# Scores' exponentials in pairs of turns: one ScalarE operation over two copied score pairs, and VectorE's exponential in other steps

## The chip, the cores and the metric

The kernel runs on one NeuronCore of a Trainium2 chip. It uses TensorE (PE; PEld is its weight load), VectorE (DVE), ScalarE (ACT), GpSimd (POOL) and the DMA queues, most of them issued from SyncE (SP). The metric is the device time of one execution in microseconds; the time before is the median of three runs, 1421.75 us (1420.74 to 1422.44).

## The reference

Two attention layers over the same shapes (2048 tokens, width 576, 32 heads of 18), their outputs side by side:

```python
def _A_ref(x, wq, wk, wv, wo):      # one key and value head for all 32 query heads
    q = heads(x @ wq); k = x @ wk; v = x @ wv
    p = softmax(q @ k.T * 18 ** -0.5)          # 32 heads x 2048 x 2048
    return concat(p @ v) @ wo
def _B_ref(x, wq, wk, wv, wo, beta):           # four segments of 512 tokens
    for s in range(4):
        p = softmax(causal(qs @ ks.T * scale))  # 32 heads x 512 x 512
        o = g * (phi(qs) @ M) / (phi(qs) @ z + 1e-6) + (1 - g) * (p @ vs)
        M, z = M + phi(ks).T @ vs, z + sum(phi(ks))
    return concat(o) @ wo
return concatenate([a, b], axis=-1)
```

The work of this case is A's softmax: 32 heads x 2048 x 2048 exponentials of fp32 scores.

## The kernel before

A first stage projects both inputs to queries, keys and values, splits them into exact parts and stores them in DRAM. It ends about 290 us into the span. All that follows is one long schedule written out by hand for PE, ACT and DVE (`manual_schedule`): each of these engines executes in the order in which the program text issues, and waits in place.

**Blocks.** A's work is cut into 32 blocks (4 chunks of 512 queries by 8 groups of 4 heads). B's is cut into 32 blocks too (segment and group of 4 heads), placed in pairs behind certain A blocks: `after` lists the A block behind which each of 16 pairs stands, and the pairs stand behind blocks 0, 1, 2, 3, 4, 8, 9, 10, 12, 16, 17, 18 and 20 (two pairs behind 0, 1 and 3). From block 21 on, A blocks follow each other.

**Pairs and turns.** An A block has 16 key tiles of 128 keys. For each key tile and each pair of heads (`pr`), two matmuls (upper and lower half of the rows) make a score tile E of 128 x 2 x 512 fp32 in PSUM (`scores`, L906). Three E buffers of two banks each (`psE`) take turns. A block has 32 such score pairs; they are issued in ten turns of three and one last turn of two (`turns`). What a score pair then meets depends on its place in the turn: the first and third are read by ACT straight from PSUM (exponential into P, L937); the middle one is copied by DVE into W in SBUF (L934), which frees its E buffer, and ACT takes its exponential from W last in the turn. In the last turn of two the second is the copied one. B's blocks have two turns of three each.

One score pair of each A block (key tile 0, `pr` 1, the middle of turn 0) gets its exponential from DVE alone (`exponentials`, L886): a first operation reads E, and eight more steps of 128 x 1024 each follow, one a turn (`slow`), skipped in turns where a block's output is read. Its result PD is used late, at place 12 of its pair's 16 key tiles (`LATE`).

**One turn** issues, in this order: the scores of its pairs (PE) with copies (DVE), the exponentials (ACT: first, third, middle), one fill step (PE: a few matmuls of an output projection into F, L770, or of B's memory, L826, with a copy to osb or o by DVE now and then), a DVE step, and the products of the turn two before (PE: P with V into O, L967; three half pairs a turn). A block's end adds a copy of O (oe, L976) and its store. `due` issues work on weights, sums and loads whose time has come.

**Tiles.** P has 9 buffers, W 2 (one pair each), PD, n, q one each (128 x 1024); stacks of queries (`load_stackA`): st0 for the first, then stA with 2 buffers, each for two blocks, asked for when the one before begins.

**Tail.** After the last block, A's last two output projections run from halves that ACT and DVE make of the weighted heads into P tiles (`halve_heads`), 3.2 us of PE for each of ten.

Of the kernel before, what the change touches and what calls it, by code (L numbers as in the profile page):

```python
# [1 line left out]

# [5 lines left out]
F32 = mybir.dt.float32  # L8
F32R = mybir.dt.float32r
BF = mybir.dt.bfloat16  # L10
I32 = mybir.dt.int32
AF = mybir.ActivationFunctionType
ALU = mybir.AluOpType
AX = mybir.AxisListType
# [4 lines left out]
S, D, H, DH = 2048, 576, 32, 18  # L19
NSEG, L = 4, 512  # L20
C = 512
NCH = S // C
NKT = S // 128
# [21 lines left out]


LOG2 = SCALE * 1.4426950408889634
ROUND = 1.5 * 2.0 ** 23
POLY = [753.2113037109375, 522.0861206054688, 180.93731689453125, 41.808597564697266, 7.287727355957031]
C5_BITS = 984482944.0  # L50

BY_DVE = ((0, 1),)
LATE = (12,)
QALL = [(slice(0, 36, 2), 0), (slice(1, 36, 2), 1), (slice(36, 54), 0)]
CA = 618
# [16 lines left out]
def attention_pair_kernel(ctx, tc, a_xT, a_w, a_wo, b_xT, b_w, b_wo, b_beta, ident_d, hmask_d, bmask_d, cmask_d, sel_d, zmask_d, selx_d, sely_d, out):  # L72
# [813 lines left out]

    def exponentials(p, e):

        n = pp.tile([128, 2, 512], F32, name="n", bufs=1)
        q = pp.tile([128, 2, 512], F32, name="q", bufs=1)  # L890
        v = nc.vector
        v.tensor_scalar(p, e, LOG2, -116.0, op0=ALU.mult, op1=ALU.max)
        steps = [
            lambda: v.tensor_scalar(n, p, ROUND, ROUND, op0=ALU.add, op1=ALU.subtract),
            lambda: v.tensor_tensor(p, p, n, op=ALU.subtract),
            lambda: v.scalar_tensor_tensor(q, p, POLY[4], p, op0=ALU.add, op1=ALU.mult),
        ]
        for a in POLY[3:0:-1]:
            steps.append(lambda a=a: v.scalar_tensor_tensor(q, q, a, p, op0=ALU.add, op1=ALU.mult))  # L899
        steps += [  # L900
            lambda: v.tensor_scalar(n.bitcast(I32), n, 2.0 ** 23, C5_BITS, op0=ALU.mult, op1=ALU.add),
            lambda: v.scalar_tensor_tensor(p, q, POLY[0], n, op0=ALU.add, op1=ALU.mult),
        ]
        slow.extend((now[0] + 2 + i, p, step) for i, step in enumerate(steps))

    def scores(it, pr, copied):  # L906

        ab, c, hg, kt = it
        st = stacks[ab, c, hg // 2]
        h = 2 * (hg % 2) + pr  # L910
        e = psE.tile([128, 2, 512], F32, name="E")
        dve = ab == "A" and (kt, pr) in BY_DVE
        p = pp.tile([128, 2, 512], F32, name="PD" if dve else "P", bufs=1 if dve else PBUFS)
        state[it, pr] = p
        n = 512 if ab == "A" else 512 - 128 * kt if kt < 2 else 384
        if ab == "A":
            for j, r0 in enumerate(HALF):
                rows = slice(r0, r0 + KR)
                nc.tensor.matmul(e[:, j], kstA[rows, 128 * kt : 128 * kt + 128], st[rows, h, :], start=True, stop=True)  # L919
            if (kt, pr) in BY_DVE:  # L920
                exponentials(p, e)
                return lambda: None
        else:
            for k, c0 in BKEYS[kt]:
                ks = slice(128 * k, 128 * k + 128)
                for j, r0 in enumerate(HALF):
                    rows = slice(r0, r0 + KR)
                    nc.tensor.matmul(  # L928
                        e[:, j, c0 : c0 + 512 - 128 * k], st[rows, 4 + h, ks], st[rows, h, 128 * k :], start=True, stop=True
                    )  # L930
        src = e
        if copied:
            src = pp.tile([128, 2, 512], F32, name="W", bufs=2)
            nc.vector.tensor_copy(src[:, :, :n], e[:, :, :n])  # L934

        def exponential():
            nc.scalar.activation(p[:, :, :n], src[:, :, :n], AF.Exp, scale=SCALE)  # L937
# [76 lines left out]
    def due(k, most=2, heavy=2):  # L1014

        cost = 0

        near = [its[n][0] for t in turns[k : k + 3] for n, pr in t]
# [68 lines left out]
    with tc.manual_schedule(engines={ENG.PE, ENG.Activation, ENG.DVE}):  # L1087
# [1 line left out]


        for n, b in enumerate(blocks):
            ms = [m for m in range(len(its)) if block_of[m] == n]
            items = [(m, k) for m in ms for k in range(2)]
            for out_, cut in ((turns, len(items) // 3), (prods, len(items) // 3 - 2)):
                at_ = split(len(items), cut)
                out_ += [items[a:z] for a, z in zip(at_, at_[1:])]
        at(ASK + 4, 0, lambda: True, lambda k: load_qf(2))

        def halve(hi, lo, src):
# [10 lines left out]
        wparts = []  # L1110
        for k in range(len(turns) + 2):
            now[0] = k
            exps = [scores(its[n], pr, i == 1) for i, (n, pr) in enumerate(turns[k])] if k < len(turns) else []
            for i in (0, 2, 1) if len(exps) == 3 else range(len(exps)):
                exps[i]()
            if memory is None:
                run_fill()
            elif k >= ASK and all(its[n][0] == "A" for n, pr in turns[k]) and next(memory, None) is None:
# [12 lines left out]
            due(k)  # L1131
            if k == len(turns):
                halve_w(0)
            for n, pr in turns[k] if k < len(turns) else []:
# [17 lines left out]

        def halve_heads(key, t):
            R = RT[t]
            x = halves_of[key, t] = pp.tile([128, 2, 512], F32R, name="P", bufs=PBUFS)
            halve(x[:R, 0], x[:R, 1], parts[key][:R, t])

        def multiply(key, t, dst):
# [25 lines left out]
        for n, key in enumerate(rows):  # L1184
            end = key == rows[-1]
            banks = [psE.tile([128, 2, 512], F32, name="E") for _ in range(3)]
            dst = [bk[:, hf, :288] for bk in banks for hf in range(2)]
            dst += [psO.tile([128, C], F32, name=nm)[:, :288] for nm in ("O", "F")]
            for t in range(5):
                while end and weighed[key] <= t:  # L1190
                    due(k, 4)
                    k += 1
                if end and t == 4:
                    halve_heads(key, t)
                multiply(key, t, dst)
            for i in range(4):
                if end:
                    osb = pp.tile([128, 2, 512], F32, name="P", bufs=PBUFS)[:, :, :288]
                elif i < 2:
                    osb = pp.tile([128, 2, 512], F32, name="W", bufs=2)[:, :, :288]  # L1200
# [62 lines left out]
```

## Time and profile before

| what | value |
|---|---|
| median of three runs | 1421.75 us |
| span of the profiled execution | 1419.2 us |
| first and last exponential of scores (L937) | 292.0 and 1376.8 us |
| exponentials by ACT from E, from W | 800, 384 |
| copies of scores by DVE (L934) | 384 |
| busy share of PE, ACT, DVE, POOL | 99%, 85%, 73%, 18% |

The profiled execution took 1419.2 us from its first to its last instruction; the runs' median is 2.55 us above that, and any sum made on the trace is carried over with this difference. Rows of a timeline read: start in us from the span's beginning, length in us, engine, line, operation, what it writes and reads, how many were merged (x2: two operations, the length from the first's start to the last's end), and in brackets how long the engine sat idle before it and what ended that. Rows of waits read: engine and line, what it waited for: us in total, times, longest. Rows of groups read: busy us, mean ns of one, then idle us before them by releaser. A matmul's end is modelled, so a turn on PE is best measured from start to start.

### The profile page before, as it was taken

What the parts mean: (1) busy time and instruction counts of PE and PEld (TensorE: products, weight loads), DVE (VectorE), ACT (ScalarE), POOL (GpSimd) and SP (SyncE); (2) the same over time, 40 slices, a digit from 0 to 9 for tenths busy, and PEclk for the clock granted to TensorE, in tenths of its full rate; (3) what the DMA queues carried; (4) which work ended last, traced back from release to release, by engine and by line L of the source; (5) the groups of instructions that cost most, each with busy time, mean ns of one, the idle gap of its engine ahead of it and who ended that gap; (6) DMA issues with size and microseconds to landing.
All of it is one profiled execution on the core that took longest, in us unless ns stands there. A gap on an engine that the chain in (4) does not pass through costs nothing.

```text
span 1419.2 us, 40029 instructions
## 1 busy us (share of the span) xinstructions
PE 1403.0 (99%) x17132; PEld 843.0 (59%) x17132; DVE 1034.8 (73%) x1221; ACT 1205.2 (85%) x1447; POOL 249.8 (18%) x326
## 2 busy tenths in 40 slices
PE   9999999999999999999999999999999999999998
PEld 6788888745555555555555555555555555555558
DVE  6656456467787778777777888777778877887773
ACT  4543434489999999999999999999999999999991
POOL 2431000003313214231110160131012400100002
PEclk9999999999999999999999999999999999999999
DMA  9766547457574535332312543232104121110013
GB/s 282 254 218 187 166 146 220 167 171 219 157 211 159 172 113 165 91 109 77 111 58 69 167 129 91 70 107 73 51 34 135 64 75 47 59 44 18 9 60 111
DMA packets 90720, 172.63 MB, mean 122 GB/s; under 512 B 14576, under 2 KB 22889, under 8 KB 90110
## 3 DMA queue, kind: packets, MB, share of 16 engines
q1 hardware_dynamic: 84122, 160.01, 36.0%
q0 software_dynamic: 1664, 4.78, 1.3%
q10 hardware_dynamic: 4752, 5.24, 1.1%
q8 instruction: 135, 2.21, 0.7%
q14 instruction: 47, 0.39, 0.1%
HBM read 99.32 MB, written 70.67 MB: 120 GB/s over the span
## 4 chain that ended last, share of the span: by engine, by line
PE 67%; ACT 9%; issue 2%; DVE 1%; DMA 0%; POOL 0%; ACTq 0%; DVEq 0%
PE O L967 30%; PE E L919 20%; PE F L770 11%; ACT P L937 9%; PE E L928 3%; PE E L1164 2%; PE F L826 1%; DVE W L934 0%; DMA oA<-oe 0%; PE F L1164 0%; PE O L1164 0%; DMA sm<-oA 0%; POOL P L942 0%; DVE osb L794 0%; DVE o L831 0%
## 5 line engine op out<-in xcount | busy, mean ns | idle before, releaser
L937 ACT ACTIVATE P<-E 128x1024 f32<-128x1024 f32 (+1 forms) x800 | 783.8, 1066 | 11.8 <-PE E L919 11.7
L934 DVE COPY W<-E 128x1024 f32<-128x1024 f32 (+1 forms) x384 | 461.1, 1201 | 178.7 <-PE E L919 121.6
L967 PE MATMUL O<-P,VA 128*32 128x256 f32 x7936 | 508.3, 379 | 0.0
L937 ACT ACTIVATE P<-W 128x1024 f32<-128x1024 f32 (+1 forms) x384 | 429.2, 1118 | 3.6 <-DVE W L934 3.4
L967 PEld LDWEIGHTS O<-P,VA 128*32 128x32 f32 x7936 | 262.5, 110 | 146.5 <-issue 5.7
L919 PE MATMUL E<-stA,kstA 56*128 56x512 f32 x1920 | 329.1, 439 | 2.0 <-DVE W L934 1.0
L919 PEld LDWEIGHTS E<-stA,kstA 56*128 56x128 f32 x1920 | 154.8, 184 | 178.3 <-ACT P L937 114.0
L942 POOL TENSOR_SCALAR_AFFINE_SELECT P<-P 128x256 f32<-128x256 f32 (+1 forms) x192 | 94.7, 493 | 474.2 <-ACT P L937 441.7
L758 POOL TENSOR_TENSOR o<-o,rb 126x512 f32<-126x512 f32 (+1 forms) x55 | 85.5, 1573 | 408.0 <-PE E L919 156.2
L770 PE MATMUL F<-woB,o 126*32 126x192 f32 (+1 forms) x1920 | 127.4, 338 | 0.3 <-DVE osb L794 0.3
L899 DVE SCALAR_TENSOR_TENSOR q<-q,PD 128x1024 f32<-128x1024 f32 x96 | 119.3, 1243 | 0.0
L967 PE MATMUL O<-P,vseg 128*32 128x256 f32 (+2 forms) x1536 | 81.4, 344 | 0.0
L770 PEld LDWEIGHTS F<-woB,o 126*32 126x32 f32 (+1 forms) x1920 | 38.2, 108 | 70.5 <-issue 62.7
L976 DVE COPY oe<-O 128x512 f32<-128x512 f32 x64 | 44.3, 692 | 40.2 <-PE O L967 39.5
L249 PE MATMUL pj<-xh,wBl 128*126 128x512 f32 x180 | 72.4, 403 | 0.0
L249 PE MATMUL pj<-xh,wBh 128*126 128x512 f32 x180 | 71.8, 400 | 0.0
L118 ACT CAST qp<-pj 126x512 fp32r<-126x512 f32 (+1 forms) x54 | 30.9, 584 | 46.6 <-DVE kmB L447 32.6
L770 PE MATMUL F<-woA,o 126*32 126x192 f32 (+1 forms) x960 | 63.9, 338 | 0.0
L928 PE MATMUL E<-stB 56*128 56x256 f32 (+3 forms) x512 | 61.8, 347 | 1.7 <-ACT P L937 1.1
L967 PEld LDWEIGHTS O<-P,vseg 128*32 128x32 f32 x1536 | 48.9, 109 | 24.1 <-issue 1.6
L119 DVE TENSOR_TENSOR qp<-pj,qp 126x512 fp32r<-126x512 f32 (+1 forms) x54 | 36.6, 685 | 35.8 <-ACT qp L118 35.7
L928 PEld LDWEIGHTS E<-stB 56*128 56x128 f32 x512 | 38.6, 185 | 32.1 <-ACT P L937 22.4
(194 smaller groups left out, 1401.9 us busy)
## 6 DMA issues: line engine op xcount, KB each, us to landing
stB<-kB SPq DMA_DIRECT2D x96, 144.0 KB
stB<-qB SPq DMA_DIRECT2D x32, 288.0 KB
stA<-qA SPq DMA_DIRECT2D x30, 288.0 KB
oA<-oe SPq DMA_DIRECT2D x32, 256.0 KB
oB<-oe SPq DMA_DIRECT2D x32, 256.0 KB
qA<-qp SPq DMA_DIRECT2D x16, 504.0 KB
kB<-qp SPq DMA_DIRECT2D x16, 504.0 KB
qB<-qp SPq DMA_DIRECT2D x16, 504.0 KB
```

Of the source, the lines that this page charges most:

```text
L119: hold(nc.vector.tensor_tensor(qp[:R, 1, :n], src, qp[:R, 0, :n].bitcast(F32), op=ALU.subtract))
L249: nc.tensor.matmul(dst, w[:, c0 : c0 + M], x, start=i == 0, stop=i == len(ops) - 1)
L758: return lambda: tc.keep_in_program_order(nc.gpsimd.tensor_tensor(dst, a, b, op=op))
L770: nc.tensor.matmul(dst[32 * j : 32 * j + 32], parts[ab, c][: RT[t], t, r0 : r0 + 32], wo[ab][: RT[t], t, c0 : c0 + n], start=start, stop=stop,
L899: steps.append(lambda a=a: v.scalar_tensor_tensor(q, q, a, p, op0=ALU.add, op1=ALU.mult))
L919: nc.tensor.matmul(e[:, j], kstA[rows, 128 * kt : 128 * kt + 128], st[rows, h, :], start=True, stop=True)
L928: nc.tensor.matmul(e[:, j, c0 : c0 + 512 - 128 * k], st[rows, 4 + h, ks], st[rows, h, 128 * k :], start=True, stop=True)
L934: nc.vector.tensor_copy(src[:, :, :n], e[:, :, :n])
L937: nc.scalar.activation(p[:, :, :n], src[:, :, :n], AF.Exp, scale=SCALE)
L942: nc.gpsimd.affine_select(diag, diag, pattern=[[0, 2], [0, m], [1, 128]], base=0, channel_multiplier=-1, compare_op=ALU.is_ge, fill=0.0)
L967: nc.tensor.matmul(o[32 * j : 32 * j + 32, q0 : q0 + n], v, p[:, j % 2, p0 : p0 + n], start=m == hf == 0, stop=last and hf == 1,)
L976: nc.vector.tensor_copy(osb, o)
```

## The change

The turns of an A block are written out by kind. Key tiles are taken in threes (i, i+1, i+2), two turns for each: the first has (i, pair 0), (i+2, pair 0), (i, pair 1); the second (i+1, pair 0), (i+2, pair 1), (i+1, pair 1). The middle ones are still copied by DVE, but into the two halves of one W of 128 x 4 x 512, and one ACT operation of 2048 columns takes both exponentials into the tile PW (4 x 512), last in the second turn. The third key tile of the first three (2) gives one pair to DVE's exponential (role "D", now `pr` 0, the middle of turn 0) and one that is copied and has a 1024-column exponential of its own. The last turn of two (key tile 15) has both pairs read from PSUM by ACT (role "E"). B's turns keep their order; their middle pairs lie in halves of W and PW too, with an exponential each.

In ACT's order, a block's exponentials before: two in turn 0, three in turns 1 to 9 (E, E, W), two in turn 10 (E, W). After: two (E, E) in turn 0, three (E, E, W) in turn 1, two in turns 2, 4, 6 and 8, two and a 2048-column one in turns 3, 5, 7 and 9, two (E, E) in turn 10. In DVE's order, nine copies a block for ten; DVE's exponential is one operation on 1024 columns and twelve on 512 (of these four are bit operations on whole words, eight have two operands), issued in groups of 3, 2, 3, 2 and 2, in turns 0, 2, 3, 4 and 5. On PE, the products of the moved key tiles change place; number and order of scores, fills and products by turn stay.

P has 6 buffers for 9; W and PW have 2 of two pairs each; n and q have half the size; st0 serves every second stack and stA has one buffer. In the tail four of the halves stand in PW.

```diff
-PBUFS = 9
+PBUFS = 6
-BY_DVE = ((0, 1),)
+BY_DVE = ((2, 0),)
 LATE = (12,)
...
-        st = pp.tile([128, 4, C], F32R, name="stA", bufs=2)
+        st = st0 if q4 % 2 == 0 else pp.tile([128, 4, C], F32R, name="stA", bufs=1)
...
     def exponentials(p, e):
...
+        u, w = (pp.tile([128, 512], F32, name=nm, bufs=1) for nm in "nq")
+        v, stt = nc.vector, nc.vector.scalar_tensor_tensor
+        v.tensor_scalar(p.bitcast(U32), e, EXP_A, EXP_B, op0=ALU.mult, op1=ALU.add)
+        ops = []
+        for t in (p[:, 0], p[:, 1]):
+            y = t.bitcast(U32)
+            ops += [
+                lambda y=y: v.tensor_scalar(u.bitcast(U32), y, MANTISSA, ONE_BITS, op0=ALU.bitwise_and, op1=ALU.bitwise_or),
+                lambda y=y: v.tensor_scalar(w.bitcast(U32), y, EXPONENT, None, op0=ALU.bitwise_and),
+                lambda t=t: stt(t, u, POLY[0], u, op0=ALU.add, op1=ALU.mult),
+                lambda t=t: stt(t, t, POLY[1], u, op0=ALU.add, op1=ALU.mult),
+                lambda t=t: stt(t, t, POLY[2], t, op0=ALU.add, op1=ALU.mult),
+                lambda t=t: stt(t, t, POLY[3], w, op0=ALU.add, op1=ALU.mult),
+            ]
+        for i, (lo, hi) in enumerate(((0, 3), (3, 5), (5, 8), (8, 10), (10, 12))):
+            slow.append((now[0] + 2 + i, p, ops[lo:hi]))
+
+    box = {}
 
-    def scores(it, pr, copied):
+    def scores(it, pr, role):
...
+        if role in (0, 1):
+            if role == 0:
+                box["W"] = pp.tile([128, 4, 512], F32, name="W", bufs=2)
+                box["P"] = pp.tile([128, 4, 512], F32, name="PW", bufs=2)
+            w, p = (box[nm][:, 2 * role : 2 * role + 2] for nm in "WP")
...
-        if copied:
-            src = pp.tile([128, 2, 512], F32, name="W", bufs=2)
+        if role in (0, 1):
+            src = w
             nc.vector.tensor_copy(src[:, :, :n], e[:, :, :n])
+            if ab == "A" and kt != BY_DVE[0][0]:
+                both = [box[nm] for nm in "PW"]
+                return (lambda: nc.scalar.activation(*both, AF.Exp, scale=SCALE)) if role else lambda: None
...
+            if b[0] == "A":
+                for i in range(0, NKT - 1, 3):
+                    x = "D" if i + 2 == BY_DVE[0][0] else 0
+                    turns.append([(m0 + i, 0, "E"), (m0 + i + 2, 0, x), (m0 + i, 1, "E")])
+                    turns.append([(m0 + i + 1, 0, "E"), (m0 + i + 2, 1, 0 if x else 1), (m0 + i + 1, 1, "E")])
+                turns.append([(m0 + NKT - 1, 0, "E"), (m0 + NKT - 1, 1, "E")])
+            else:
+                turns.append([(m0, 0, "E"), (m0, 1, 0), (m0 + 1, 0, "E")])
+                turns.append([(m0 + 1, 1, "E"), (m0 + 2, 0, 1), (m0 + 2, 1, "E")])
...
-            exps = [scores(its[n], pr, i == 1) for i, (n, pr) in enumerate(turns[k])] if k < len(turns) else []
+            exps = [scores(its[n], pr, role) for n, pr, role in turns[k]] if k < len(turns) else []
             for i in (0, 2, 1) if len(exps) == 3 else range(len(exps)):
                 exps[i]()
...
-                slow.pop(0)[2]()
+                for op in slow.pop(0)[2]:
+                    op()
```

More of the change, by code (lines that the diff above doesn't have):

```diff
@@ L1 @@
+import math
 from contextlib import ExitStack, nullcontext
@@ L11 @@
 I32 = mybir.dt.int32
+U32 = mybir.dt.uint32
 AF = mybir.ActivationFunctionType
@@ L887, in exponentials @@
     def exponentials(p, e):
[L889 to L904, printed above, removed]
-    def scores(it, pr, copied):
+        u, w = (pp.tile([128, 512], F32, name=nm, bufs=1) for nm in "nq")
[16 more added lines that the diff above has]
+    def scores(it, pr, role):
         ab, c, hg, kt = it
@@ L911, in scores @@
         e = psE.tile([128, 2, 512], F32, name="E")
-        dve = ab == "A" and (kt, pr) in BY_DVE
-        p = pp.tile([128, 2, 512], F32, name="PD" if dve else "P", bufs=1 if dve else PBUFS)
+        if role in (0, 1):
[4 more added lines that the diff above has]
+        else:
+            dve = role == "D"
+            p = pp.tile([128, 2, 512], F32, name="PD" if dve else "P", bufs=1 if dve else PBUFS)
         state[it, pr] = p
@@ L919, in scores @@
                 nc.tensor.matmul(e[:, j], kstA[rows, 128 * kt : 128 * kt + 128], st[rows, h, :], start=True, stop=True)
-            if (kt, pr) in BY_DVE:
+            if role == "D":
                 exponentials(p, e)
@@ L1016, in due @@
         cost = 0
-        near = [its[n][0] for t in turns[k : k + 3] for n, pr in t]
+        near = [its[t[0][0]][0] for t in turns[k : k + 3]]
         heavy *= "B" not in near
@@ L1091, in attention_pair_kernel @@
         for n, b in enumerate(blocks):
[L1092 to L1096, printed above, removed]
+            m0 = block_of.index(n)
+            if b[0] == "A":
[4 more added lines that the diff above has]
+                turns.append([(m0 + NKT - 1, 0, "E"), (m0 + NKT - 1, 1, "E")])
+            else:
+                turns.append([(m0, 0, "E"), (m0, 1, 0), (m0 + 1, 0, "E")])
+                turns.append([(m0 + 1, 1, "E"), (m0 + 2, 0, 1), (m0 + 2, 1, "E")])
+            halves = [(m, hf) for m in range(len(its)) if block_of[m] == n for hf in range(2)]
+            at_ = split(len(halves), len(halves) // 3 - 2)
+            prods += [halves[a:z] for a, z in zip(at_, at_[1:])]
         at(ASK + 4, 0, lambda: True, lambda k: load_qf(2))
@@ L1117, in attention_pair_kernel @@
                 run_fill()
-            elif k >= ASK and all(its[n][0] == "A" for n, pr in turns[k]) and next(memory, None) is None:
+            elif k >= ASK and its[turns[k][0][0]][0] == "A" and next(memory, None) is None:
                 memory = None
@@ L1133, in attention_pair_kernel @@
                 halve_w(0)
-            for n, pr in turns[k] if k < len(turns) else []:
+            for n, pr, role in turns[k] if k < len(turns) else []:
                 it = its[n]
@@ L1154, in halve_heads @@
             R = RT[t]
-            x = halves_of[key, t] = pp.tile([128, 2, 512], F32R, name="P", bufs=PBUFS)
+            if key == rows[0] or t == 4:
+                x = pp.tile([128, 2, 512], F32R, name="P", bufs=PBUFS)
+            else:
+                if t % 2 == 0:
+                    box["x"] = pp.tile([128, 4, 512], F32R, name="PW", bufs=2)
+                x = box["x"][:, 2 * (t % 2) : 2 * (t % 2) + 2]
+            halves_of[key, t] = x
             halve(x[:R, 0], x[:R, 1], parts[key][:R, t])
@@ L1199, in attention_pair_kernel @@
                 elif i < 2:
-                    osb = pp.tile([128, 2, 512], F32, name="W", bufs=2)[:, :, :288]
+                    osb = pp.tile([128, 4, 512], F32, name="W", bufs=2)[:, :2, :288]
                 else:
```

7 lines of the change are left out of this document (4 added, 3 removed).

## The prediction

> **What bounds the kernel now.** I read the page's head first, then the busy time by stretches, then the waits of one regular stretch, and last the two timelines of one block.
>
> ```profile
> span 1419.2 us, 40029 instructions
> ```
> ```profile
> 1113.00:1346.00 233.00, 232.91 (x3287) 121.77 (x3276) 184.98 (x180) 231.03 (x250) 10.13 (x8) 1.00 0.13 40
> ```
> ```profile
> PEld E L919 <- ACT P L937: 19.8, 57, 0.4
> ...
> ACT P L937 <- PE E L919: 1.5, 6, 0.3
> ```
>
> The second row covers eight A blocks (length, then busy time of PE, PE's weight loads, DVE, ACT, POOL; clock; DMA): PE is busy 232.91 of 233.00 us and ACT 231.03. Clock and DMA are out of it. The waits of 1172 to 1346 us show that two engines share the bound: PE waits 57 times for an exponential to give a score buffer back, ACT six times, once a block, for scores. So the order of two chains decides, not a sum of busy times. One block on each:
>
> ```profile
> 1201.14 1.21 PE L919 MATMUL E<-stA,kstA 56*128 56x512 f32 x6
> 1202.27 0.53 PE L770 MATMUL F<-woA,o 72*32 72x192 f32 x8
> ...
> 1204.03 0.96 PE L919 MATMUL E<-stA,kstA 56*128 56x512 f32 x6
> 1204.92 0.53 PE L770 MATMUL F<-woA,o 126*32 126x192 f32 x8
> ...
> 1206.68 0.97 PE L919 MATMUL E<-stA,kstA 56*128 56x512 f32 x6
> ...
> 1223.64 0.53 PE L770 MATMUL F<-woA,o 126*32 126x192 f32 x8
> ...
> 1226.42 0.53 PE L770 MATMUL F<-woA,o 126*32 126x192 f32 x8
> ...
> 1228.18 0.73 PE L919 MATMUL E<-stA,kstA 56*128 56x512 f32 x4
> ...
> 1230.17 1.17 PE L919 MATMUL E<-stA,kstA 56*128 56x512 f32 x6
> ```
> ```profile
> 1201.28 1.21 ACT L937 ACTIVATE P<-W 128x1024 f32<-128x1024 f32 x1
> 1202.23 2.09 ACT L937 ACTIVATE P<-E 128x1024 f32<-128x1024 f32 x2
> 1204.57 1.94 ACT L937 ACTIVATE P<-E 128x1024 f32<-128x1024 f32 x2 [0.25 <-PE E L919]
> 1206.40 1.06 ACT L937 ACTIVATE P<-W 128x1024 f32<-128x1024 f32 x1
> 1207.35 1.94 ACT L937 ACTIVATE P<-E 128x1024 f32<-128x1024 f32 x2
> 1209.15 1.08 ACT L937 ACTIVATE P<-W 128x1024 f32<-128x1024 f32 x1
> ...
> 1223.88 2.06 ACT L937 ACTIVATE P<-E 128x1024 f32<-128x1024 f32 x2
> ```
>
> Read the constants off these rows. **PE:** a turn that waits for nothing takes 2.65 us (1204.03 to 1206.68): 0.90 from its scores to its fill (F), 1.76 from fill to the next scores. The short last turn takes 1.99 (1228.18 to 1230.17). **ACT:** by their ends (1206.51, 1207.46, 1209.29) exponentials follow each other at 0.915 us from PSUM and 0.945 from W. Scores that begin when ACT is free end their first exponential 1.57 us later (1204.03 to 1206.51 less one 0.915). **Handover:** PE's fill at 1226.42 comes 0.48 us after the exponential that ended at 1225.94, on whose buffer the turn's third scores waited.
>
> With these constants a block goes turn by turn: fill = the later of scores + 0.90 and the previous turn's last PSUM exponential + 0.48; next scores = fill + 1.76; first exponential ends at the later of the preceding exponential's end + 0.915 and scores + 1.57. For the kernel before, started with its own 1.13 us from scores to fill and a last exponential that ends at 1202.49 (1.35 into the block), this gives 29.00 us; the rows give 29.03. The steps therefore describe this kernel, and I use them on the new one.
>
> **The change, part by part.**
>
> *Wide exponentials.* The rest of ACT's price per instruction comes from two sizes:
>
> ```profile
> 904.23 1.68 ACT L937 ACTIVATE P<-E 128x768 f32<-128x768 f32 x2
> 905.62 1.03 ACT L937 ACTIVATE P<-W 128x768 f32<-128x768 f32 x1
> ```
>
> Two exponentials of 768 columns follow at 0.695 us each, against 0.90 for 1024 by starts (1207.35 to 1209.15, two): 0.82 ns a column, 0.84 us per 1024. So 0.105 of W's 0.945 us is fixed, and I take 0.945 + 0.84 = 1.79 us for 2048 columns. No row shows that size; the ends are 1.70 (no fixed part) and 1.89 (nothing saved). Four an A block save 0.42 us of ACT, the block's last middle pair read from PSUM instead of W another 0.03: 0.45 a block, 14 over 32 blocks.
>
> The Trainium skill (Perfetto Trace Analysis, Optimizing Scalar/DVE Operations) gives 93 ns for ScalarE's fixed part on SBUF and says that grouping helps a saturated engine; by it the wide operation would take 1.80, and the block below would be some 0.03 us longer, as an estimate. The trace agrees on the size. The same section says that long instructions on an engine that causes bubbles elsewhere are better broken up; that is this forecast's case.
>
> *When ACT's work falls due.* This is the part that decides. A block's turns gave ACT 2, 3, 3 ... 3, 2 exponentials. Now turn 0 has 2, turn 1 has 3, turn 2 has 2, turn 3 has 2 and the wide one at its very end, and so on in twos. Over turns 0 to 3 ACT has about nine short operations for four PE turns, so it must idle; what it hasn't done comes back as wide operations later, and ACT is late when the block ends.
>
> *The last turn.* It was (E, copy): DVE freed the second score buffer at once. Now both pairs of key tile 15 are exponentials from PSUM, queued behind the wide operation of turn 9. With three buffers in rotation, turn 0 of whatever follows reuses, for its third scores, the buffer of that very last exponential. PE issues in order, so its fill and products queue behind, and ACT then starves in turn 1.
>
> The same steps, with the new kinds of turn (A block after A block, settled so that it starts as the last ended; us from its first scores):
>
> | turn | scores | fill | last PSUM exp | end of ACT's turn |
> |---|---|---|---|---|
> | 0 | 0.00 | 1.70 | 3.05 | 3.05 |
> | 1 | 3.46 | 4.36 | 5.94 | 6.89 |
> | 2 | 6.12 | 7.02 | 8.72 | 8.72 |
> | 3 | 8.78 | 9.68 | 11.26 | 13.05 |
> | 5 | 14.10 | 15.36 | 16.71 | 18.50 |
> | 7 | 19.78 | 20.81 | 22.27 | 24.06 |
> | 9 | 25.23 | 26.37 | 27.72 | 29.51 |
> | 10 | 28.13 | | 31.34 | 31.34 |
>
> The next block starts at 28.13 + 1.99 = 30.12; its fill is at 31.34 + 0.48, that is 1.70 into it, where this one began. PE loses 0.80 in turn 0 (1.70 for 0.90) and 0.7 in turns 5, 7 and 9; ACT loses about 1.05 in turn 1 (scores 3.46 + 1.57 = 5.03 against 3.05 + 0.915) and 0.7 in turn 3. Against 29.01 the block is **1.11 us longer**. At 1.70 and 1.89 for the wide operation it is 0.84 and 1.41.
>
> *Blocks with B between.*
>
> ```profile
> 954.30 0.96 PE L919 MATMUL E<-stA,kstA 56*128 56x512 f32 x6
> ...
> 978.09 1.14 PE L928 MATMUL E<-stB 56*128 56x512 f32 x6
> 979.16 0.53 PE L770 MATMUL F<-woB,o 72*32 72x192 f32 x8
> ...
> 980.92 0.84 PE L928 MATMUL E<-stB 56*128 56x384 f32 x10
> ```
> ```profile
> 954.34 1.06 ACT L937 ACTIVATE P<-W 128x1024 f32<-128x1024 f32 x1
> ```
>
> A block that follows B has its first two turns as before. From turn 2 (954.30, ACT free at 955.40) the steps give a last exponential at 979.52, so the fill of B's first turn at 980.00 instead of 979.16. From fill to B's next scores are the bare 1.76 (979.16 to 980.92), so PE is the bound there and the **0.84 us** (0.57 to 1.14) stays.
>
> ```profile
> 418.50 0.91 PE L928 MATMUL E<-stB 56*128 56x384 f32 x10
> 419.34 1.50 PE L967 MATMUL O<-P,VA 128*32 128x256 f32 x24
> ```
>
> The B pairs after the first three A blocks have no fill (products follow scores directly); PE has room, ACT is the bound and gains some 0.3 us each.
>
> *VectorE.* By block it loses one copy and changes its own exponential:
>
> ```profile
> L934 DVE COPY W<-E 128x1024 f32<-128x1024 f32 x352 | 430.4, 1223 | 141.5 <-PE E L919 121.6 <-PE E L928 11.3 <-ACT P L937 6.2
> ...
> L976 DVE COPY oe<-O 128x512 f32<-128x512 f32 x64 | 44.3, 692 | 40.2 <-PE O L967 39.5
> ...
> L894 DVE TENSOR_SCALAR n<-PD 128x1024 f32<-128x1024 f32 x32 | 23.8, 743 | 0.8
> ```
>
> A copy of 512 columns costs 0.69 against 1.22 for 1024, so each two-operand step of 512 is put at 0.69; the bit operations, never shown, lie between 0.37 (half of L894) and 0.69, and I take 0.37, the nearest row being of their kind. Per turn that is 1.22 for the copy and 1.38 to 1.43 for the steps, 2.6 to 2.65 in a turn of 2.65 or more: hidden, barely. At 0.69 it isn't (a rival below).
>
> *Buffers.* Six P, two PW of two pairs and the two stacks are enough: a P is rewritten three turns on, after the products two turns on, which PE has passed by then; a stack is asked for when the one two back has had its last scores. Loads, fills and products keep their number and place, and the tail's halves and output rows only change the buffers that they stand in, after the last turn: 0.
>
> **Sum.** Thirteen of the 31 joints between A blocks hold B pairs, so 18 blocks pay 1.11 (20.0), ten joints with fill pay 0.84 (8.4), three gain 0.3 (-0.9): +27.5. The span goes from 1419.2 to 1446.7. The median of the runs lies 2.55 us above the span (1421.75), so I predict **1449 us**; with the ends of the wide operation's price 1442 to 1458.
>
> **Rivals.** (1) *ACT's saving counts*: if the handover of turn 0's third buffer came early enough, ACT would be the one chain and the 14 us would show: 1408. It decides by the end of the last exponential: at 0.42 us or less into the next block PE waits for nothing; I find 1.22, and in the kernel before 1.35, but on a W that holds no score buffer. For it: ACT at 231.03 of 233.00. Against it: PE has only 233.00 less 232.91, and its bare turns add up to 10 x 2.65 + 1.99 = 28.5 a block, so half a microsecond a block is the most there is, and any wait takes from it. (2) *The two cancel*: the lateness moves into ACT's present idle time; 1421. Against it: that is one 0.25 us gap a block. (3) *VectorE too*: with bit operations at 0.69 a turn of copy, three steps and now and then an osb copy takes 3.3 us, the wide operation of turn 5 waits some 0.6 us for its copy, and 32 blocks add 19: 1468.
>
> **How the numbers follow.** Forecast 0.72, ACT's saving 0.11, cancelled 0.05, VectorE too 0.12. The 80% range takes in the forecast with some 8 us under its lower end for joints that hide part of the wait, and rival 3: 1434 to 1468. A measurement tells about 0.2% (2.8 us) from no change, so faster 0.11, same 0.05, slower 0.84.
>
> **What would show it.** At block starts the fill about 1.7 us after the first scores, with PE's weight load waiting for ACT; ACT then idle about 1 us before turn 1; wide operations at 1.8 us from end to end; block period near 30.1 where 29.0 stood. A period of 28.5 would show rival 1, waits of ACT for DVE's W rival 3. I am wrong if PE's third scores of turn 0 don't wait.

## The result and the profile after

The changed kernel takes **1471.67 us** (median of four runs, 1470.63 to 1473.82) against 1421.24 us for the kernel before beside it (1420.67 to 1422.44): a ratio of 1.0354 [1.034, 1.0369]. It is slower, as forecast, but by 50 us instead of 27, and lies above the end of the range.

The page of the changed kernel, its span, its busy time and its chain by engine; below it the chain of the kernel before:

```profile
span 1469.3 us, 40025 instructions
PE 1423.8 (97%) x17132; PEld 846.5 (58%) x17132; DVE 962.8 (66%) x1317; ACT 1204.7 (82%) x1319; POOL 238.6 (16%) x326
PE 41%; ACT 28%; issue 5%; DVE 4%; DMA 1%; SPq 0%; POOL 0%; ACTq 0%; DVEq 0%
```
```profile
PE 67%; ACT 9%; issue 2%; DVE 1%; DMA 0%; POOL 0%; ACTq 0%; DVEq 0%
```

ACT was 9% of the chain and is now 28%: PE waits for it far more often. DVE is on the chain with 4% though it is busy for less of the span than before (66% for 73%). That is the first sign that not only ACT's order counts.

Two A blocks of the changed kernel by stretch (length; busy PE, PE's weight loads, DVE, ACT, POOL; clock; DMA share, GB/s), a quiet one and a long one:

```profile
1213.26:1243.48 30.22, 29.57 (x412) 15.24 (x408) 20.06 (x25) 28.58 (x28) 0.00 (x0) 1.00 0.07 22
...
834.53:869.06 34.53, 31.26 (x412) 15.82 (x408) 26.58 (x25) 28.91 (x28) 20.35 (x14) 0.95 0.43 133
```

The quiet block takes 30.22 us. The long one has the same instructions on PE, DVE and ACT and takes 4.3 us more; DVE's 25 instructions are busy 6.5 us longer, and GpSimd works for 20 us in it.

**The quiet block** on PE and on ACT, from both timelines:

```profile
1213.26 0.87 PE L930 MATMUL E<-st,kstA 56*128 56x512 f32 x4
1214.56 0.50 PE L930 MATMUL E<-st,kstA 56*128 56x512 f32 x2 [0.42 <-ACT P L951]
1214.99 0.53 PE L773 MATMUL F<-woA,o 126*32 126x192 f32 x8
...
1228.27 0.50 PE L930 MATMUL E<-st,kstA 56*128 56x512 f32 x2 [0.19 <-ACT P L951]
```
```profile
1217.35 1.94 ACT L951 ACTIVATE P<-E 128x1024 f32<-128x1024 f32 x2 [1.01 <-PE E L930]
...
1222.66 1.94 ACT L951 ACTIVATE P<-E 128x1024 f32<-128x1024 f32 x2 [0.60 <-PE E L930]
...
1226.28 3.77 ACT L951 ACTIVATE P<-E 128x1024 f32<-128x1024 f32 x4
1229.90 1.95 ACT L948 ACTIVATE PW<-W 128x2048 f32<-128x2048 f32 x1
```

All marks that the prediction named are there. The third scores of turn 0 wait for an exponential, and the fill comes 1.73 us after the first scores (1213.26 to 1214.99; worked out as 1.70). ACT then idles 1.01 before turn 1 and 0.60 before turn 3 (1.05 and 0.7). The wide operation costs 1.80 from end to end (1226.28 + 3.77 = 1230.05 to 1231.85; taken as 1.79). PE waits again for ACT in turn 5.

**The joint with B**, on PE from the first B block behind an A block on, in the changed kernel and then before, and ACT in the A block that follows B in the changed kernel:

```profile
794.60 0.88 PE L939 MATMUL E<-stB 56*128 56x512 f32 x4
795.90 0.44 PE L939 MATMUL E<-stB 56*128 56x384 f32 x2 [0.41 <-ACT P L951]
...
800.56 0.92 PE L939 MATMUL E<-stB 56*128 56x512 f32 x6
...
805.28 0.98 PE L930 MATMUL E<-st,kstA 56*128 56x512 f32 x6
```
```profile
774.49 1.12 PE L928 MATMUL E<-stB 56*128 56x512 f32 x6
...
779.84 0.90 PE L928 MATMUL E<-stB 56*128 56x512 f32 x6
```
```profile
809.69 1.03 ACT L951 ACTIVATE P<-E 128x1024 f32<-128x1024 f32 x1 [0.23 <-PE O L981]
```

The first B block is 5.96 us long for 5.35, by the same wait for the same late exponential. The last row is another wait: the scores of this exponential were there (they began at 807.84), but ACT stood 0.23 us for products (O), which read the P tile that it writes next. The changed kernel's trace has 22 such waits, 5.7 us in all; the trace of before has none.

**The long block** on DVE, GpSimd and PE:

```profile
842.62 0.68 DVE L902 SCALAR_TENSOR_TENSOR PD<-PD,n 128x512 f32<-128x512 f32 x1
...
846.31 1.63 DVE L904 SCALAR_TENSOR_TENSOR PD<-PD,q 128x512 f32<-128x512 f32 x1
847.87 1.50 DVE L899 TENSOR_SCALAR n<-PD 128x512 uint32<-128x512 uint32 x1
849.29 1.49 DVE L900 TENSOR_SCALAR q<-PD 128x512 uint32<-128x512 uint32 x1
850.70 1.21 DVE L945 COPY W<-E 128x1024 f32<-128x1024 f32 x1
```
```profile
843.14 3.00 POOL L761 TENSOR_TENSOR o<-o,rb 126x512 f32<-126x512 f32 x2 [4.54 <-DMA rb<-rB]
846.10 2.98 POOL L761 TENSOR_TENSOR rb<-rb 126x512 f32<-126x512 f32 x2
849.04 4.60 POOL L761 TENSOR_TENSOR o<-o,rb 126x512 f32<-126x512 f32 x3
```
```profile
849.04 0.51 PE L930 MATMUL E<-stA,kstA 56*128 56x512 f32 x2 [0.27 <-ACT P L951]
851.96 0.73 PE L930 MATMUL E<-stA,kstA 56*128 56x512 f32 x4 [2.42 <-DVE W L945]
```

Read it from the last fence back. PE stands still for 2.42 us, waiting for the copy that frees a score buffer. The copy itself isn't slow (1.21 us); it stands in DVE's queue behind three steps of the exponential, which took 1.63, 1.50 and 1.49 us. The first row shows such a step that begins before GpSimd does: 0.68. GpSimd multiplies tiles of 126 x 512 (L761) all the while. Seven of the trace's A blocks are long in this way, by 0.3 to 4.3 us against the same blocks of e3 below, where GpSimd's operations are short, and each has these multiplications in it.

The Trainium skill (SBUF — State Buffer, Who interferes with whom) says that a VectorE instruction with two SBUF inputs, or one in a two-port mode, shares a port pair with GpSimd, that the one that comes second stands until the other is done, and that a VectorE instruction with at most one SBUF input outside those modes doesn't. The trace agrees: the copy from PSUM keeps its 1.21 us beside the same GpSimd work. The prediction had not weighed it.

### The profile page after: what moved, and what is told of

It is laid out like the page before. It is cut to its first block, busy times and chain, and to the rows that moved or that the text cites. A ratio compares the mean times of both kernels' runs of the same rounds, so it can differ in the third digit from the quotient of the medians.

```text
span 1469.3 us, 40025 instructions
## 1 busy us (share of the span) xinstructions
PE 1423.8 (97%) x17132; PEld 846.5 (58%) x17132; DVE 962.8 (66%) x1317; ACT 1204.7 (82%) x1319; POOL 238.6 (16%) x326
## 3 DMA queue, kind: packets, MB, share of 16 engines
q8 instruction: 135, 2.21, 0.6%
## 4 chain that ended last, share of the span: by engine, by line
PE 41%; ACT 28%; issue 5%; DVE 4%; DMA 1%; SPq 0%; POOL 0%; ACTq 0%; DVEq 0%
ACT P L951 21%; PE O L981 18%; PE E L930 11%; ACT PW L948 6%; PE F L773 6%; PE E L939 3%; DVE W L945 2%; PE E L1193 2%; PE F L829 1%; DMA stB<-qB 1%; DVE PD L902 0%; ACT PW L951 0%; DVE PD L903 0%; PE F L1193 0%; PE O L1193 0%
## 5 line engine op out<-in xcount | busy, mean ns | idle before, releaser
L945 DVE COPY W<-E 128x1024 f32<-128x1024 f32 (+1 forms) x352 | 421.8, 1198 | 227.5 <-PE E L930 150.2
L981 PE MATMUL O<-PW,VA 128*32 128x256 f32 x2304 | 273.9, 380 | 0.5 <-ACT PW L948 0.5
L948 ACT ACTIVATE PW<-W 128x2048 f32<-128x2048 f32 x128 | 246.3, 1924 | 6.4 <-DVE W L945 6.4
L930 PE MATMUL E<-stA,kstA 56*128 56x512 f32 x1024 | 183.3, 443 | 19.4 <-DVE W L945 11.0
L930 PE MATMUL E<-st,kstA 56*128 56x512 f32 x1024 | 184.7, 446 | 10.7 <-ACT P L951 8.0
L930 PEld LDWEIGHTS E<-stA,kstA 56*128 56x128 f32 x1024 | 83.6, 185 | 121.2 <-ACT P L951 85.7
L930 PEld LDWEIGHTS E<-st,kstA 56*128 56x128 f32 x1024 | 84.1, 185 | 112.7 <-ACT P L951 92.7
L761 POOL TENSOR_TENSOR o<-o,rb 126x512 f32<-126x512 f32 (+1 forms) x55 | 78.8, 1448 | 429.0 <-DMA o<-oA 152.9
L981 PEld LDWEIGHTS O<-PW,VA 128*32 128x32 f32 x2304 | 119.8, 110 | 33.8 <-ACT PW L948 3.3
L951 ACT ACTIVATE PW<-W 128x1024 f32<-128x1024 f32 (+1 forms) x96 | 96.1, 1001 | 4.0 <-DVE W L945 3.8
L981 PE MATMUL O<-P,vseg 128*32 128x192 f32 (+2 forms) x1024 | 81.6, 340 | 0.3
```

Of the source, the lines that this page charges most:

```text
L761: return lambda: tc.keep_in_program_order(nc.gpsimd.tensor_tensor(dst, a, b, op=op))
L948: return (lambda: nc.scalar.activation(*both, AF.Exp, scale=SCALE)) if role else lambda: None
L981: nc.tensor.matmul(o[32 * j : 32 * j + 32, q0 : q0 + n], v, p[:, j % 2, p0 : p0 + n], start=m == hf == 0, stop=last and hf == 1,)
```

## The experiments

My theory after the result: three costs add up, (a) pairing the copied scores makes ACT's work fall due late in the block, (b) the last turn read from PSUM holds turn 0's third score buffer, as forecast, and (c) VectorE's bunched steps are held up by GpSimd. The rivals: the wide operation itself is the cost; the steps are simply too much work for VectorE; or it is (b) alone, larger than worked out.

### The last turn's second pair copied again (e1)

```diff
-            if ab == "A" and kt != BY_DVE[0][0]:
+            if ab == "A" and kt not in (BY_DVE[0][0], NKT - 1):
...
-                turns.append([(m0 + NKT - 1, 0, "E"), (m0 + NKT - 1, 1, "E")])
+                turns.append([(m0 + NKT - 1, 0, "E"), (m0 + NKT - 1, 1, 0)])
```

> The changed kernel, but the second score pair of each A block's last turn is copied to W by VectorE again and has its own 1024-column exponential from there. Theory (buffer): the third score buffer comes back with the copy, so the fill of the next block's first turn falls back from 1.7 to about 1.0 us; the steps of the prediction give 29.5 us for an A block after an A block (30.2 measured with the change, 29.0 before) and take some 0.6 us off each joint with B, together about -19 us on 1471.7: 1453. What stays over the time before is ACT's idle time in turns 1 and 3 and VectorE's lateness. Rival (VectorE is what costs): another copy a block makes VectorE later still: 1472 or more.

Measured 1468.31 us, ratio 1.0329 [1.0311, 1.0346]: almost no gain, which taken alone speaks for the rival. But quiet A blocks went to 29.55 and first B blocks to 5.27, as (b) says. The gain went into the second B blocks, 6.02 instead of 4.7. There DVE, ACT and PE read:

```profile
1084.96 1.23 DVE L945 COPY W<-E 128x1024 f32<-128x1024 f32 x1 [0.64 <-PE E L939]
```
```profile
1088.53 1.06 ACT L951 ACTIVATE PW<-W 128x1024 f32<-128x1024 f32 x1 [1.67 <-PE O L981]
```
```profile
1087.84 0.62 PE L981 MATMUL O<-PW,VA 128*32 128x256 f32 x8
```

The copy was done at 1086.19, but ACT stood 1.67 us for products (O) to read PW before it could be written again: my edit needed a third PW tile, and only two exist. So the edit added a wait of its own; e5 takes it out.

### The same, with the exponential into P (e5)

```diff
+        if role == "C":
+            src = pp.tile([128, 4, 512], F32, name="W", bufs=2)[:, 0:2]
+            nc.vector.tensor_copy(src, e)
...
+                turns.append([(m0 + NKT - 1, 0, "E"), (m0 + NKT - 1, 1, "C")])
```

> As e1_last_copied, but the exponential of the copied last pair goes to a P tile instead of a PW tile. In e1 the blocks came out as the theory said (29.55 us for an A block after an A block, first B block 5.28 instead of 5.96), but each second B block rose from 4.7 to 6.03: its exponential into PW waited, with the copy long done, for products that read the PW tile of two turns of pairs before. Theory (buffer): with P that goes, and the last turn's copy gives back its whole worth, 18 x 0.67 + 13 x 0.68: about 21 us off 1471.7, 1451. Rival (the third buffer was a small matter, PW tells nothing): 1468 as in e1.

Measured 1454.79 us, 1.0234 [1.0219, 1.025]: 17 us better than the changed kernel. The rows of a B pair on PE:

```profile
1071.52 1.05 PE L939 MATMUL E<-stB 56*128 56x512 f32 x6
...
1076.80 0.90 PE L939 MATMUL E<-stB 56*128 56x512 f32 x6
...
1081.51 0.73 PE L930 MATMUL E<-st,kstA 56*128 56x512 f32 x4
```

The first B block is back to 5.28 and the second to 4.71, quiet A blocks take 29.53. The last turn's buffer is (b), and with the other costs in place it is worth 17 us, where 21 had been expected.

### The pairs without the wide operation (e2)

```diff
-            if ab == "A" and kt != BY_DVE[0][0]:
+            if False:
```

> The changed kernel, but each copied pair has its own 1024-column exponential in its own turn; the halves of W and PW, the last turn and VectorE's steps stay as changed. Theory (two causes): even turns have three exponentials again, ACT's idle time in turn 3 and PE's waits in turns 5, 7 and 9 go, the wait in turn 0 stays (last exponential of the block still holds the third buffer); the steps of the prediction give 29.7 for an A block after an A block, 0.5 less than measured, so about -9 on the 18 of them and little at the joints with B: about 1461. Rival (the wide operation is the whole loss): back to 1425.

Measured 1464.4 us, 1.0309 [1.0291, 1.0326]. The start of a block on PE:

```profile
1207.65 0.96 PE L930 MATMUL E<-st,kstA 56*128 56x512 f32 x4
1209.03 0.49 PE L930 MATMUL E<-st,kstA 56*128 56x512 f32 x2 [0.42 <-ACT P L951]
1209.46 0.53 PE L773 MATMUL F<-woA,o 126*32 126x192 f32 x8
```

The fill still comes 1.81 us after the scores: the wait belongs to the order of the last turn, not to the wide operation. Quiet A blocks are 29.73, half a microsecond shorter than with the wide operation, although ACT is busy for a little longer in them (28.72 us for 28.58). So in these blocks the grouped operation saves a little of ACT's time and costs more of the block's. A blocks behind B don't follow: they take 29.05, against 29.13 with the wide operation and 28.67 before. Their lengthening is nearly all there without it, and so are the waits for P (22, 5.7 us).

### GpSimd's multiplications cut to 8 columns (e3), and VectorE's steps left out (e4)

```diff
-            return lambda: tc.keep_in_program_order(nc.gpsimd.tensor_tensor(dst, a, b, op=op))
+            return lambda: tc.keep_in_program_order(nc.gpsimd.tensor_tensor(dst[:, :8], a[:, :8], b[:, :8], op=op))
```

> The changed kernel with GpSimd's weighing of the heads cut to 8 of 512 columns (the other columns stay unweighted, part of the computation is left out). Theory: the trace shows VectorE's 512-column steps at 1.6 us instead of 0.69 while a GpSimd operation of line 761 runs, and eight or so blocks 1 to 5 us longer than their like in just these stretches; without those operations these blocks return to 30.2 or 29.1 us and the kernel gets about 14 us faster: 1458. Rival: the long blocks have another cause (DMA, loads): 1471.

```diff
-            slow.append((now[0] + 2 + i, p, ops[lo:hi]))
+            pass
```

> The changed kernel with VectorE's exponential cut to its first operation (the twelve steps on 512 columns are left out, so one score pair a block has no true exponential). Theory: VectorE is late only where its steps meet GpSimd, so the same 14 us go as without the weighing, or a few more because the copy of turn 3 is no longer late in any block; the regular period falls at most from 30.2 to 30.1: 1455 to 1458. Rival (VectorE is nearly full in each turn, so its steps cost in every block): 25 us or more.

Measured 1457.68 us, 1.026 [1.0243, 1.0277], and 1453.97 us, 1.0231 [1.0214, 1.0248]. One of VectorE's steps by its source line (least, median and longest ns), in the changed kernel and then in e3, and e3's block starts on PE around the place of the long block:

```profile
L903 DVE SCALAR_TENSOR_TENSOR PD<-PD x64: 674/691/1662, 298.3 to 1414.0; 128x512 f32<-128x512 f32 x64
```
```profile
L903 DVE SCALAR_TENSOR_TENSOR PD<-PD x64: 678/691/695, 297.8 to 1398.1; 128x512 f32<-128x512 f32 x64
```
```profile
829.29 0.87 PE L930 MATMUL E<-stA,kstA 56*128 56x512 f32 x4
...
859.50 0.87 PE L930 MATMUL E<-stA,kstA 56*128 56x512 f32 x4
...
889.72 0.88 PE L930 MATMUL E<-st,kstA 56*128 56x512 f32 x4
```

With GpSimd's operations short, the longest step falls from 1662 to 695 ns, the median stays, and the block of 34.53 us takes 30.21, like the next (30.22). All long blocks are gone and 14 us with them. Leaving the steps out altogether brings 3.7 us more, with intervals that touch, and quiet blocks stay at 30.22: the steps are not too much work, they are work that gets held up.

### VectorE's new exponential alone, in the kernel before (e6)

Its edit is the new `exponentials` and the loop that issues a group of steps; turns, W, P and the last turn are those of before.

> The kernel before with the changed kernel's VectorE exponential alone (one operation on 1024 columns and twelve on 512 instead of nine on 1024), turns and copies as before. Theory (more VectorE operations on SBUF, each of which can be held up for about 1 us by a GpSimd operation): the few long blocks come back, 8 to 14 us: 1429 to 1435, and in undisturbed blocks nothing changes (29.0 and 28.7). Rival (the steps are harmless with the old turns, where a late copy has a turn's slack on ScalarE): 1421.

Measured 1436.69 us, 1.0098 [1.0076, 1.012]: 15 us, somewhat above what I expected. Quiet blocks are as before (29.00), six are 1.5 to 4.0 us longer than the same blocks before, the longest 33.07. DVE in one of them, and in the same place of the kernel before:

```profile
834.31 1.62 DVE L904 SCALAR_TENSOR_TENSOR PD<-PD,q 128x512 f32<-128x512 f32 x1
835.85 1.51 DVE L899 TENSOR_SCALAR n<-PD 128x512 uint32<-128x512 uint32 x1
837.28 1.48 DVE L900 TENSOR_SCALAR q<-PD 128x512 uint32<-128x512 uint32 x1
838.69 1.21 DVE L937 COPY W<-E 128x1024 f32<-128x1024 f32 x1
```
```profile
824.01 1.77 DVE L896 SCALAR_TENSOR_TENSOR q<-PD 128x1024 f32<-128x1024 f32 x1
825.71 1.21 DVE L934 COPY W<-E 128x1024 f32<-128x1024 f32 x1
```

The kernel before is held up too (1.77 us where such a step otherwise takes 1.21 to 1.24), but one step at a time, with a copy behind each. In e6 three short steps stand in a row, and each loses about a microsecond before the copy gets its turn.

### Number of steps or their kind (e10), and what the hold-ups cost before (e8)

e10 computes the new formula in the kernel before in six steps of 1024 columns, one a turn, bit operations included. e8 is the kernel before with e3's edit.

```diff
+            lambda: v.tensor_scalar(u.bitcast(U32), y, MANTISSA, ONE_BITS, op0=ALU.bitwise_and, op1=ALU.bitwise_or),
+            lambda: v.tensor_scalar(w.bitcast(U32), y, EXPONENT, None, op0=ALU.bitwise_and),
+            lambda: stt(p, u, POLY[0], u, op0=ALU.add, op1=ALU.mult),
...
+            lambda: stt(p, p, POLY[3], w, op0=ALU.add, op1=ALU.mult),
```

> The kernel before with the same six steps on 1024 columns, one a turn, its score pair in turn 0 as before. It tells what in e6 cost 15 us. Theory (the number of steps and their bunching, two and three in one turn, each held up for about 1 us by GpSimd): with six steps, one a turn, no block is longer than before: 1421, perhaps 1 to 2 less. Rival (the bit operations on whole words or the in-place steps are what GpSimd holds up): 1430 or more.

> The kernel before with GpSimd's weighing cut to 8 of 512 columns (the other columns stay unweighted, part of the computation is left out). Theory: before, VectorE had eight operations of the kind that GpSimd holds up and a middle exponential came last in every turn, so few copies came too late; its long blocks (29.3 to 29.4 us instead of 29.0 or 28.7, and one turn of 3.9) add up to some 3 us: 1418. Rival (the hold-ups cost the kernel before just as much): 1407.

Measured 1420.16 us, 0.9999 [0.999, 1.0008], and 1420.74 us, 0.9995 [0.9986, 1.0005]. The same arithmetic one step a turn costs nothing: it is the twelve small steps in bunches that cost 15 us. And the hold-ups cost the kernel before nothing that can be measured, where 3 us had been expected, so there is nothing to win there.

### Pairing alone (e12)

e5 with e3's edit: pairs and wide operations, the last turn's second pair copied as before, no hold-ups. The smaller sets of buffers of the change (six P for nine) are still in it, and so is the later place of VectorE's pair.

> e5 (last pair copied) with GpSimd's weighing cut to 8 of 512 columns (the other columns stay unweighted, part of the computation is left out): of the change, only the pairing of turns with its wide exponentials is left to cost anything. Theory (three separate costs: hold-ups 14, last turn 17, pairing the rest): an A block after an A block 29.53 for 29.01, one after B 29.11 for 28.67, first B blocks as before, so 18 x 0.52 + 10 x 0.44 + some 2 at the start: 16 us, 1437 to 1438. Rival (the costs overlap, pairing alone costs nothing once VectorE is on time): 1421 to 1426.

Measured 1437.12 us, 1.0108 [1.0087, 1.013]. Block starts on PE:

```profile
1214.88 1.10 PE L930 MATMUL E<-stA,kstA 56*128 56x512 f32 x6
...
1244.41 1.10 PE L930 MATMUL E<-stA,kstA 56*128 56x512 f32 x6
```

An A block takes 29.53 for 29.0. Pairing, with all that the wide operations save and with six P buffers, is 15 to 16 us slower than the kernel before. How this divides was not tried: no run has the pairs with nine P buffers, or six P buffers with the old turns. In A blocks behind A, e2 puts the half microsecond down to the wide operation. In those behind B the lengthening begins at the waits for P: in the block at 792.62 the third and fourth turns, right behind such a wait, take 2.78 and 2.77 us, for 2.66 and 2.65 in the same block before (784.54).

### Looking for a better order (e7, e9, e11)

Here the kernel before gives VectorE a score pair later in the block, so that its first operation, which holds a score buffer, falls away from the block's start. e9 does the same with e10's six steps, e11 with e3's edit.

```diff
-BY_DVE = ((0, 1),)
-LATE = (12,)
+BY_DVE = ((6, 1),)
+LATE = (15,)
```

> The kernel before with VectorE's score pair moved from the middle of turn 0 to the middle of turn 4 (key tile 6, second pair, used last of its 16); nothing else changes. The steps of the prediction: the last turn and turn 0 no longer follow each other with two exponentials each, ScalarE doesn't run dry in turn 1, PE waits less at the block's start, and an A block after an A block takes 28.78 instead of 29.02 us; 18 of these give -4 us, joints with B perhaps another -1: 1416. Rival (the bound is PE's bare work, ScalarE's gap was free): 1421.

> The kernel before with the changed kernel's formula for VectorE's exponential, but on all 1024 columns (one operation on the scores and six steps, one a turn, instead of eight), and its score pair in the middle of turn 4 as in e7. In e7 undisturbed blocks got shorter (28.9 for 29.0, 28.45 for 28.67, first B block 5.14 for 5.36), and some eight blocks 0.3 to 1.6 us longer. Theory (VectorE's steps meeting GpSimd's operations took the gain back): with two steps fewer and one a turn, most of the long blocks go and 18 x 0.1 + 10 x 0.43 + a little, 5 to 7 us, show: 1415. Rival (the later place itself makes the long blocks): 1421 to 1423 as in e7.

> e7 (VectorE's pair in turn 4, old steps) with GpSimd's weighing cut to 8 of 512 columns (the other columns stay unweighted, part of the computation is left out). Theory (hold-ups took e7's gain): all its long blocks go and the gain of the undisturbed blocks shows, 6 to 8 us: 1414. Rival: 1421.

Measured 1423.07 us, 1.0008 [0.9999, 1.0017]; 1421.6 us, 1.0004 [0.9995, 1.0013]; 1419.25 us, 0.9991 [0.9982, 1.0]. All three miss their expectations of five to seven microseconds. The local gain is there: in e7 quiet A blocks take 28.90 (1176.90 to 1205.80) for 29.0, and those behind B 28.45 for 28.67. It is given back elsewhere. In e7 part of that is hold-ups again, as in this row of PE in a block of 30.52:

```profile
1118.93 0.49 PE L919 MATMUL E<-stA,kstA 56*128 56x512 f32 x2 [0.75 <-DVE W L934]
```

Without hold-ups (e11) these long blocks go, but some blocks of 29.2 to 29.6 remain, and the blocks up to 460 us are 1.2 us longer together. Why these give the rest back wasn't tried and stays open. No version here beats the kernel before by more than the measurement can tell.

## Why the prediction was right in its sign and wrong in its size

Taking the parts away one after another splits the 50 us: 1471.67 to 1457.68 without hold-ups (14.0), to 1437.12 with the last turn as before (20.6), to 1421.24 without the pairs (15.9). Put on in the other order, the steps alone cost 15.4 (e6), pairs 18.1 more (e5), the last turn 16.9 more: the same three costs, each within 4 us.

1. **The bound and its constants: right.** The recurrence gave 1.70 us from scores to fill and a block of 30.12; the trace has 1.73 and 30.22. The agreement for the kernel before was in part put in: started from its own 1.13 and 1.35 the steps give 29.0, but settled as the new kernel was, each block starting as the last ended, they give 28.80.
2. **Wide operation: its price right, with some luck.** 1.79 worked out, 1.80 measured. The rows quoted (0.90 us for 1024 columns, 0.695 for 768) give 0.80 ns a column, not 0.82, and so 1.77. The saving hardly shows: ACT is busy 28.58 us of a quiet block for 28.78 before, and just as long from the first scores to those of the last A block (1042.3 us for 1042.1), where 14 us less had been worked out. Why the sum doesn't fall stays open.
3. **ACT's order and the last turn: right.** A block's 1.11 was 1.2: in e3, where nothing is held up, the 17 A blocks behind A are 20.5 us longer together, with 20.0 forecast for 18. e5 and e12 show that the two causes named, pairs and last turn, are two causes.
4. **Joints with B: a quarter too small.** I had 0.84; the trace has 0.46 in the A block behind B (29.13 for 28.67) and 0.60 in the first B block, 1.06. Over ten joints that is 2 us. By the prediction's own steps the A block behind B gets only 0.2 us longer; in the block at 805.28 the third and fourth turns alone are 0.24 longer than before, behind the wait for P (item 7).
5. **Joints without fill: wrong.** I gave them a gain of 0.3 us each, because ACT, which bounds there, has less to do. The stretch up to about 460 us is 4 us longer in e3 and in e12 alike: in e12 its first A block takes 29.48 for 27.79, the next three 30.05, 30.44 and 30.40 for 29.37, 29.92 and 29.46. ACT bounds there only as long as it never waits. Before, it ran through the second A block with no gap until the block's end; in e12 it stands there four times, 1.24 us together: 0.63 for products to have read a P tile (at 344.69), the rest for scores.
6. **VectorE, "hidden, barely": the step that failed.** Its durations were nearly right, two-operand steps 0.69 and bit operations 0.42 (414 to 420 ns; I took 0.37). But I added up quiet durations, left out the copy to osb (0.34 us) that stands in some turns, concluded that a turn of 2.6 to 2.65 us of work fits into 2.65 us, and put VectorE into the sum at nothing. With GpSimd at work most steps take 1.5 to 1.66 us, three in a row take 4.5 (846.31 to 850.78), and the copy behind them holds PE. That is 14 us, the larger part of the 23 us by which the forecast was short. The profile before already had the sign, in the longest of the steps of its own exponential (least, median, longest ns):

```profile
L899 DVE SCALAR_TENSOR_TENSOR q<-q,PD x96: 1207/1215/2098, 301.0 to 1365.8; 128x1024 f32<-128x1024 f32 x96
```

7. **Buffers: wrong in part.** PW and the stacks were enough; six P were not. I had PE past a P tile's products before ACT writes it again; in the trace ACT waits 22 times for them, in the second B block of a pair and in the A block behind it. At 0.24 us a joint, as in item 4, over thirteen joints that is some 3 us of the 50, an estimate that no run tests: none has the changed kernel with nine P.

Together the hold-ups (14.0), the joints without fill (4 us of loss where 0.9 of gain was put) and the ten joints (2) make 21 of the 23 us.

Rival 3 (VectorE too, 1468) comes nearest in its number, but not by its mechanism: it needed bit operations at 0.69, and they take 0.42, and it charged all 32 blocks, where seven are long. Its sign, ACT waiting for W, shows at 8 of the 128 wide operations (6.4 us; 2 and 1.1 us in e3); in the long block PE's own wait for the copy comes first. Rivals 1 and 2 are refuted: no A block behind an A block takes 28.5 or 29.0.

## What to carry to other kernels

Where two engines hand buffers to each other in fixed order, grouping an engine's operations can cost more than their overhead: ask when each result falls due and which buffer its queue holds, and let a recurrence of the waits, not a sum of busy times, give the block. Work that is "just hidden" must be priced with its neighbours at work: look in the trace for the longest of each instruction, not only for its mean, and ask who else was busy then. Here six steps, one between two copies, cost nothing, and twelve shorter ones in groups of two and three cost 15 us.

## What the runs showed of the hardware

VectorE's SBUF operations of 128x512 fp32 went from 0.69 us to between 1.63 and 1.66, and bit operations from 0.42 to 1.50, while GpSimd multiplied 126x512 tiles from SBUF at about 1.5 us each (843.14 to 846.10 for two); copies from PSUM beside them stayed at 1.21. Not every step was caught: those that began at 851.83 and 855.25, right behind a copy, took 0.68 with GpSimd at work.

A long block can cost more than the wait itself. The stretches of the changed kernel around the 2.42 us pause of PE, and of e6 around a pause of 2.72 us (837.23 to 839.95):

```profile
849.00:852.00 3.00, 0.54 (x4) 0.22 (x4) 3.00 (x4) 1.81 (x2) 3.00 (x4) 1.00 0.56 186
852.00:855.80 3.80, 3.80 (x37) 1.66 (x37) 3.77 (x4) 1.47 (x2) 3.39 (x3) 0.62 0.33 119
```
```profile
837.00:840.00 3.00, 0.28 (x4) 0.05 (x2) 3.00 (x4) 0.34 (x2) 2.88 (x3) 1.00 0.53 175
840.00:843.80 3.80, 3.80 (x54) 2.08 (x58) 3.73 (x6) 3.80 (x5) 2.29 (x2) 1.00 0.39 137
```

In the changed kernel, after three microseconds in which PE was busy for 0.54, its granted clock was 0.62 over the next 3.8 us, and pairs of products took 0.65 us for their usual 0.39. So a pause of 2.4 us was followed by a slower turn as well. It isn't always so: in e6 the longer pause was followed by a clock of 1.00, and so was one of 2.21 us in the changed kernel (985.34 to 987.55). What decides it no run here shows.
